# Batch 0's first DFT stage on four 64x64 tiles, and the array between the two stages stored in the order in which it is made

## The chip, the core and the metric

The kernel runs on one NeuronCore of one Trainium2 chip. The metric is the device time of one execution in microseconds (us), less is better. "Before" is the kernel without the change.

## What is computed

A frequency-domain layer feeds a feed-forward layer with a rational activation. Cut to what matters:

```python
# x: (4, 3008, 256); w_r, w_i: (256, 256); moe_w_in: (256, 2048); moe_w_out: (2048, 256)
X = np.fft.rfft(x, axis=1)
Yr = Xr @ w_r - Xi @ w_i + b_r
Yi = Xr @ w_i + Xi @ w_r + b_i
Y = soft_threshold(Yr, 0.01) + 1j * soft_threshold(Yi, 0.01)
x2 = np.fft.irfft(Y, n=3008, axis=1).reshape(12032, 256)
h = x2 @ w_in
g = (a0 + a1*h + a2*h**2 + a3*h**3) / (1 + |b0|*|h| + |b1|*h**2 + 1e-6)
out = g @ w_out
```

## The kernel before

The transform of length 3008 is split as 47 x 64, and done with matmuls for each of the four batches:

- **Stage f1** (`f1_first` for batch 0, `f1_task` for the others) is a DFT of length 47 over `n2`, for each of the 64 values of `n1`. `n1` is cut into two groups of 32 (`NG`, `NJ`), and each group into eight chunks of four (`c`). A chunk `xin` holds 2 x 47 rows (each padded to 48) by 4 x 256 columns. Its result `a` goes to `s1`, an array in DRAM.
- **Stage f2** (`f2_task`) reads `s1` back with another axis on the partitions (`load_all` into `b_all` for batch 0, `load_b` for the others): 128 partitions are 2 (real, imaginary) x 64 values of `n1`. It is a matmul with the table `f2`, 24 planes `k` in 12 pairs `p`. Batch 0's loads of `b_all` wait for all stores of `s1`, since each plane has rows from every chunk.
- **Mix** (`m_task`), soft threshold, and the **inverse stages** (`i1_task` to DRAM array `s2`, `i2_task`) follow.
- The **feed-forward part** is the main loop over 208 units `u` (26 blocks of 4 or 5 x 94 tokens, 8 units each), lines L460 (first product) to L553 (second product). The transforms of batches 1 to 3 are interleaved with it by a budget of costs.

Batch 0's transform is the prologue, written out by hand. All loads and stores of it are issued on SP's queue in program order; only `f1o`, batch 0's first table, is issued on ACT's. In order: nine warming matmuls on a tile of zeros (`warm(9)`, L625), the eight loads of `xin` (L152), four small loads (`load_small`, L636 to L640), the 16 steps of `f1_first` with a store of `a` after every second one (L187), two loads (`load_f2(0, 8)`, eight planes of the table `f2`, and `load_wt`, the mixing weights `wt`), three loads of `b_all`, more table loads, and the first raw weights of the feed-forward part (`more_raw`). `warm(WARM)`, 33 matmuls, keeps TensorE at work between the two stages. Then comes the loop over `p`, in which `f2_task`, `m_task` and `i1_task` of different `p` follow each other, with steps of `convert` between them: it turns raw 64-bit weights into pairs of 32-bit ones, 16 jobs of five steps (ACT, VectorE, GpSimd). `HC` and `HM` say how many steps stand after `f2_task` and after `m_task` of each `p`, and `HF` how many after the five first-stage tasks of batch 1 behind the loop.

`f1_first` uses one 96 x 128 table, block-diagonal over the two groups, so that one matmul does both groups for two of the four columns of a chunk. `f1_task` uses a 64 x 64 table at two places, and four matmuls on the four quarters of the array:

```python
        for g, h in ((0, 0), (1, 1), (0, 1), (1, 0)):
            r = slice(64 * g, 64 * g + 48)
            nc.tensor.matmul(out=pts[g][64 * h:64 * h + 64], lhsT=f1[r],
                             rhs=xin[b, c][r, 2 * h:2 * h + 2, :].rearrange("p j d -> p (j d)"), start=True, stop=True)
```

`copy(0, ...)` is ACT's, `copy(1, ...)` VectorE's (L159, L157). `bank` gives accumulator banks: two of tag `ft`, two of tag `h` during the prologue.

Of the kernel before, what the change touches and what calls it, by code (L numbers as in the profile page):

```python
# [29 lines left out]
HC = (0, 0, 3, 3, 3, 3, 3, 3, 3, 3, 3, 3)  # L30
HM = (0, 0, 3, 4, 3, 4, 3, 4, 3, 4, 3, 4, 8, 0)
HF = (2, 3, 2, 0, 0)
# [5 lines left out]
def dft_tables():  # L38
# [35 lines left out]
    f1o = np.zeros((NG, ROWS, NK, 2, NG))  # L74
    for q in range(NG):
        f1o[q, :, :, :, q] = f1
    f1o = np.pad(f1o.reshape(96, 96), ((0, 0), (0, 32)))
# [10 lines left out]
    sel[2:4, 130:] = 1.0  # L88
    f = np.float32
    return {  # L90
        "f1": f1p.astype(f),
        "f1o": f1o.astype(f),
        "i2": i2p.astype(f),
        "f2": f2.reshape(128, NK * 128).astype(f),
# [7 lines left out]
def spectral_moe(ctx, tc, t, out):  # L102
# [20 lines left out]
    wsp = {}  # L123
# [18 lines left out]
    def load_x(b, c):  # L142
# [8 lines left out]
        rows = 96 if b == 0 and c < 2 else 128  # L151
        nc.sync.dma_start(out=xt[:rows], in_=(t["x"][b - 1, c] if b else t["x0"][c])[:rows])  # L152
# [15 lines left out]
    a_t = {}  # L168

    def new_s1(b):  # L170
        s1[b] = dram.tile([NK, 2, NG, NJ, D], F32, tag="s1", name="s1")

    def f1_first(i):
        c, r = divmod(i, 2)
        if i == 0:
            new_s1(0)
        pt = bank(0, "f1" if r else "")
        nc.tensor.matmul(out=pt, lhsT=f1o, rhs=xin[0, c][:96, 2 * r:2 * r + 2, :].rearrange("p j d -> p (j d)"),  # L178
                         start=True, stop=True)
        if not r:  # L180
            a_t[0] = const.tile([128, 4, D], F32, tag=f"wsp{c}", name="a")[:96]
        copy(r, a_t[0][:, 2 * r:2 * r + 2].rearrange("p j d -> p (j d)"), pt[:96])
        if r:
            del xin[0, c]
        if r or i >= 14:
            z = slice(2 * r, 2 * r + 2) if i >= 14 else slice(0, 4)
            nc.sync.dma_start(out=s1[0].rearrange("k c g j d -> (k c g) j d")[:, 4 * c + z.start:4 * c + z.stop, :], in_=a_t[0][:, z])  # L187

    def f1_task(b, c, pos):
# [3 lines left out]
        for g, h in ((0, 0), (1, 1), (0, 1), (1, 0)):  # L193
            r = slice(64 * g, 64 * g + 48)
            nc.tensor.matmul(out=pts[g][64 * h:64 * h + 64], lhsT=f1[r],  # L195
                             rhs=xin[b, c][r, 2 * h:2 * h + 2, :].rearrange("p j d -> p (j d)"), start=True, stop=True)
# [17 lines left out]
        dst = s1[b].rearrange("k c g j d -> (k c) g j d")  # L214

        def send():
            for h in range(2):
                r, o = slice(64 * h, 64 * h + 48), slice(4 * c + 2 * h, 4 * c + 2 * h + 2)
                if whole is not None:
                    nc.sync.dma_start(out=dst[:, :, o], in_=whole[r])  # L220
                else:
                    for g in range(NG):
                        nc.sync.dma_start(out=dst[:, g, o], in_=parts[g][r])
# [7 lines left out]
    def load_b(b, p):  # L231
        bt = sm.tile([128, 2, D], F32, tag="b", name="bt")
        nc.sync.dma_start(out=bt, in_=s1[b][2 * p:2 * p + 2].rearrange("k c g j d -> (c g j) k d"))
        b_t[b, p] = bt
# [378 lines left out]
    with tc.manual_schedule():  # L613
        nc.vector.memset(cb, 1.0)
        f1o = pro.tile([96, 128], F32, tag="f1o", name="f1o", bufs=1)
        nc.scalar.dma_start(out=f1o, in_=t["f1o"])
# [79 lines left out]
        def load_all(k, m):  # L696
            nc.sync.dma_start(out=b_all[k // 6][:, k % 6:k % 6 + m], in_=s1[0][k:k + m].rearrange("k c g j d -> (c g j) k d"))
# [16 lines left out]
        for i in range(16):  # L714
            f1_first(i)
# [228 lines left out]
```

## Time and profile before

| | |
|---|---|
| time, median of 3 runs | 1415.99 us (1415.75 to 1417.21) |
| the profiled execution: its own time, its span | 1419.05 us, 1417.3 us |
| TensorE matmul busy | 1390.0 us, 98% of the span |
| VectorE, ACT, GpSimd busy | 91%, 81%, 47% |
| first matmul of f1, of f2 (batch 0) | 5.61 us, 29.65 us |

The span is the part of the profiled execution from its first to its last instruction. The runs without a profile are some 3 us shorter than the profiled one. In the views, PE is TensorE's matmul, PEld its weight load, DVE VectorE, SPq the sequencer of the SP queue; `L187` is a line of the program; `out<-in` names tiles without their numbers. "Landing" is the time from the issue of a transfer until its completion is seen.

### The profile page before, as it was taken

The page shows a single profiled execution, that of the slowest core. Times are in us where ns is not written, and L with a number is a line of the kernel's source. Part 1 is how long each engine was busy: PE and PEld are TensorE (multiplying, and loading weights), DVE is VectorE, ACT ScalarE, POOL GpSimd, SP SyncE. Part 2 cuts the span into 40 slices and gives each one's busy share as a digit, 9 for nine tenths or more (in the row PEclk, how much of TensorE's full clock was granted, in tenths as well). Part 3 has the DMA queues.
Part 4 walks back from the last instruction along what each step waited for, and adds up shares of the span by engine and source line. Part 5 has one row for each costly group of instructions (what it writes and reads, how often), then busy time and mean ns, then how long its engine had stood idle before and what let it go on. Part 6 is the DMA issues. An engine that isn't in the chain of part 4 may idle for free.

```text
span 1417.3 us, 20378 instructions
## 1 busy us (share of the span) xinstructions
PE 1390.0 (98%) x7279; PEld 1210.9 (85%) x7279; DVE 1291.5 (91%) x1304; ACT 1144.5 (81%) x1513; POOL 670.5 (47%) x444
## 2 busy tenths in 40 slices
PE   9998999999999999999999999999999999999997
PEld 4977889998878989898888899998888888888887
DVE  3779899898999989999989999999999999999998
ACT  2768887887888778888888778888888898888985
POOL 0444444444554444454545444444545555555553
PEclk9999999999999999999999999999999999999999
DMA  9966556556776556556687465656555465555543
GB/s 309 379 215 162 117 121 150 110 114 158 160 204 151 116 130 141 117 121 156 148 208 158 98 142 126 127 115 133 108 127 118 97 122 96 112 118 99 117 77 80
DMA packets 95657, 200.48 MB, mean 141 GB/s; under 512 B 10748, under 2 KB 51748, under 8 KB 95556
## 3 DMA queue, kind: packets, MB, share of 16 engines
q0 software_dynamic: 29664, 97.62, 38.0%
q1 hardware_dynamic: 65780, 101.51, 23.2%
q8 instruction: 58, 0.95, 0.3%
q14 instruction: 43, 0.35, 0.1%
q10 hardware_dynamic: 112, 0.05, 0.0%
HBM read 54.61 MB, written 37.49 MB: 65 GB/s over the span
## 4 chain that ended last, share of the span: by engine, by line
PE 72%; DVE 10%; issue 9%; ACT 5%; DMA 4%; SPq 0%; DVEq 0%; ACTq 0%
PE h L460 28%; PE acc L553 27%; PE pi L426 4%; PE pft L315 4%; DVE t L511 3%; DVE v L523 3%; PE pft L376 2%; DMA v<-s 2%; PE pft L297 2%; PE pft L255 2%; PE pft L195 1%; PE pft L178 1%; DVE g L520 1%; ACT t L499 1%; DMA s<-zt 1%
## 5 line engine op out<-in xcount | busy, mean ns | idle before, releaser
L553 PE MATMUL acc<-g,wsp 128*128 128x470 f32 (+1 forms) x2496 | 563.7, 375 | 3.4 <-DVE g L533 3.4
L527 POOL TENSOR_TENSOR t<-t,v 128x940 f32<-128x940 f32 (+1 forms) x206 | 469.7, 2280 | 164.4 <-DVE v L523 143.8
L553 PEld LDWEIGHTS acc<-g,wsp 128*128 128x128 f32 x2496 | 470.0, 190 | 62.8 <-DVE g L533 5.0
L460 PE MATMUL h<-xsh,win 128*128 128x470 f32 (+1 forms) x1664 | 436.9, 384 | 6.0 <-DVE t L512 5.6
L497 POOL DMA_DIRECT2D v<-s x206 | 181.6, 882 | 489.7 <-issue 452.9
L460 PEld LDWEIGHTS h<-xsh,win 128*128 128x128 f32 x1664 | 304.8, 189 | 61.6 <-PE acc L553 9.8
L520 DVE SCALAR_TENSOR_TENSOR g<-t,small,y 128x940 fp32r<-128x940 f32 (+1 forms) x208 | 250.3, 1203 | 45.8 <-ACT y L506 42.6
L492 ACT ACTIVATE v<-h 128x940 f32<-128x940 f32 (+1 forms) x208 | 196.2, 943 | 95.4 <-PE h L460 92.1
L511 DVE TENSOR_TENSOR t<-t,h 128x940 f32<-128x940 f32 (+1 forms) x208 | 231.3, 1112 | 27.3 <-ACT t L499 25.6
L512 DVE SCALAR_TENSOR_TENSOR t<-t,small,h 128x940 f32<-128x940 f32 (+1 forms) x208 | 245.2, 1179 | 7.4
L533 DVE SCALAR_TENSOR_TENSOR g<-t,small,y 128x940 fp32r<-128x940 f32 (+1 forms) x208 | 244.2, 1174 | 0.1
L460 PE MATMUL h<-xsl,win 128*128 128x470 f32 (+1 forms) x832 | 241.4, 371 | 0.0
L523 DVE SCALAR_TENSOR_TENSOR v<-v,g 128x940 f32<-128x940 f32 (+1 forms) x208 | 231.8, 1114 | 0.1
L504 ACT ACTIVATE y<-v 128x940 f32<-128x940 f32 (+1 forms) x208 | 206.1, 991 | 21.4 <-DMA v<-s 21.4
L499 ACT ACTIVATE t<-h,small 128x940 f32<-128x940 f32 (+1 forms) x208 | 216.2, 1039 | 0.0
L506 ACT ACTIVATE y<-y 128x940 f32<-128x940 f32 (+1 forms) x208 | 205.1, 986 | 2.0
L493 ACT ACTIVATE s<-h 128x940 f32<-128x940 f32 (+1 forms) x208 | 195.7, 941 | 0.0
L460 PEld LDWEIGHTS h<-xsl,win 128*128 128x128 f32 x832 | 155.8, 188 | 20.1
L426 PEld LDWEIGHTS pi<-small,ct 96*128 96x128 f32 x516 | 65.2, 192 | 7.9 <-ACT s L493 3.6
L426 PE MATMUL pi<-small,ct 96*128 96x94 f32 (+1 forms) x516 | 66.2, 275 | 3.5 <-DVE x L268 2.9
L159 ACT ACTIVATE pft<-offset 128x256 f32<-128x256 f32 x36 | 14.1, 391 | 57.6 <-DVE yt L321 23.3
L255 PEld LDWEIGHTS pft<-f,bt 128*128 128x128 f32 x288 | 37.3, 191 | 4.9 <-DVE yt L321 1.9
(113 smaller groups left out, 1071.0 us busy)
## 6 DMA issues: line engine op xcount, KB each, us to landing
v<-s POOLq DMA_DIRECT2D x190, 470.0 KB, 4.7
xin<-in_x SPq DMA_DIRECT2D x30, 512.0 KB, 6.4
s<-zt SPq DMA_DIRECT2D x48, 256.0 KB, 3.5
out_t<-ob SPq DMA_DIRECT2D x48, 235.0 KB, 4.5
ct<-s SPq DMA_DIRECT2D x20, 480.0 KB, 5.6
bt<-s SPq DMA_DIRECT2D x36, 256.0 KB, 3.3
y<-yt SPq DMA_DIRECT2D x144, 64.0 KB, 2.3
s<-a SPq DMA_DIRECT2D x46, 192.0 KB, 5.1
```

The source lines that it names most:

```text
L460: nc.tensor.matmul(out=h[:, i, :w], lhsT=l, rhs=r, start=k == 0, stop=k == len(halves) // FU - 1)
L492: nc.scalar.activation(out=d["v"], in_=h, func=ACTF.Abs, scale=rate["b0"])
L499: nc.scalar.activation(out=d["t"], in_=h, func=ACTF.Identity, scale=rate["a3"], bias=ca[:, 2:3])
L504: nc.scalar.activation(out=d["y"], in_=d["v"], func=ACTF.Square, bias=C0)
L506: nc.scalar.activation(out=d["y"], in_=d["y"], func=ACTF.Abs_reciprocal_sqrt)
L511: nc.vector.tensor_tensor(out=tt, in0=tt, in1=h, op=ALU.mult)
L512: nc.vector.scalar_tensor_tensor(out=tt, in0=tt, scalar=ca[:, 1:2], in1=h, op0=ALU.add, op1=ALU.mult)
L520: stt(out=hi, in0=tt, scalar=ca[:, 0:1], in1=y, op0=ALU.add, op1=ALU.mult)
L523: stt(out=v, in0=v, scalar=C0, in1=v32(hi), op0=ALU.add, op1=ALU.mult)
L527: nc.gpsimd.tensor_tensor(out=tt[:, :cut], in0=tt[:, :cut], in1=v[:, :cut], op=ALU.subtract)
L533: stt(out=lo, in0=tt, scalar=ca[:, 0:1], in1=y, op0=ALU.add, op1=ALU.mult)
L553: nc.tensor.matmul(out=acc[n][e][:, :w], lhsT=l, rhs=r, start=begun[n][e] == 1, stop=begun[n][e] == 3 * FU * UB)
```

## The change

Batch 0's first stage now does what `f1_task` does: per chunk four matmuls on quarters of the array (`f1_mm`, shared by both), two accumulator banks, one copy each by ACT and VectorE, two stores of 48 rows. The table `f1o` is gone; `f1` is loaded in its place at the start. All chunks of all batches are loaded as 112 rows (two groups of 48 at partitions 0 and 64); before, batch 0's first two loads had 96 rows and all others 128. `s1` has its 64 values of `n1` in the order in which the chunks give them, so that a store row is 4 KB in one piece, and the rows of the table `f2` are put in the same order on the host. The small loads go from SP's queue to ACT's. Of `f2`, four planes instead of eight are loaded ahead of `b_all`, and eight instead of four behind. The steps of `convert` start one `p` later and are spread anew.

```diff
-HC = (0, 0, 3, 3, 3, 3, 3, 3, 3, 3, 3, 3)
-HM = (0, 0, 3, 4, 3, 4, 3, 4, 3, 4, 3, 4, 8, 0)
-HF = (2, 3, 2, 0, 0)
+HC = (0, 0, 0, 3, 3, 3, 3, 3, 3, 3, 3, 3)
+HM = (0, 0, 0, 4, 4, 4, 4, 4, 4, 4, 4, 4, 8, 0)
+HF = (2, 3, 2, 1, 1)
...
+    order = np.arange(N1).reshape(NG, NJ // 4, 2, 2).transpose(1, 2, 0, 3).ravel()
...
-        "f2": f2.reshape(128, NK * 128).astype(f),
+        "f2": f2[:, order].reshape(128, NK * 128).astype(f),
...
-        rows = 96 if b == 0 and c < 2 else 128
-        nc.sync.dma_start(out=xt[:rows], in_=(t["x"][b - 1, c] if b else t["x0"][c])[:rows])
+        nc.sync.dma_start(out=xt[:112], in_=t["x"][b, c, :112])
...
-        s1[b] = dram.tile([NK, 2, NG, NJ, D], F32, tag="s1", name="s1")
+        s1[b] = dram.tile([NK, 2, N1, D], F32, tag="s1", name="s1")
...
-    def f1_first(i):
-        c, r = divmod(i, 2)
-        if i == 0:
-            new_s1(0)
-        pt = bank(0, "f1" if r else "")
-        nc.tensor.matmul(out=pt, lhsT=f1o, rhs=xin[0, c][:96, 2 * r:2 * r + 2, :].rearrange("p j d -> p (j d)"),
-                         start=True, stop=True)
-        if not r:
-            a_t[0] = const.tile([128, 4, D], F32, tag=f"wsp{c}", name="a")[:96]
-        copy(r, a_t[0][:, 2 * r:2 * r + 2].rearrange("p j d -> p (j d)"), pt[:96])
-        if r:
-            del xin[0, c]
-        if r or i >= 14:
-            z = slice(2 * r, 2 * r + 2) if i >= 14 else slice(0, 4)
-            nc.sync.dma_start(out=s1[0].rearrange("k c g j d -> (k c g) j d")[:, 4 * c + z.start:4 * c + z.stop, :], in_=a_t[0][:, z])
+    def f1_first(c):
+        if c == 0:
+            new_s1(0)
+        pts = [bank(0, "f1" if g else "") for g in range(NG)]
+        f1_mm(0, c, pts)
+        whole = const.tile([128, NG, 2, D], F32, tag=f"wsp{c}", name="a")
+        for g in range(NG):
+            copy(g, whole[:, g].rearrange("p j d -> p (j d)"), pts[g])
+        del xin[0, c]
+        dst = s1[0].rearrange("k c n d -> (k c) n d")
+        for h in range(2):
+            nc.sync.dma_start(out=dst[:, 8 * c + 4 * h:8 * c + 4 * h + 4], in_=whole[64 * h:64 * h + 48].rearrange("p g j d -> p (g j) d"))
...
-                    nc.sync.dma_start(out=dst[:, :, o], in_=whole[r])
+                    nc.sync.dma_start(out=dst[:, o:o + 4], in_=whole[r].rearrange("p g j d -> p (g j) d"))
...
-        nc.scalar.dma_start(out=f1o, in_=t["f1o"])
+        nc.scalar.dma_start(out=f1, in_=t["f1"])
...
-            nc.sync.dma_start(out=sel, in_=t["sel"])
+            nc.scalar.dma_start(out=sel, in_=t["sel"])
...
-                nc.sync.dma_start(out=bsb[2 * k:2 * k + 2, :],
+                nc.scalar.dma_start(out=bsb[2 * k:2 * k + 2, :],
...
-            nc.sync.dma_start(out=eye, in_=t["minus"])
+            nc.scalar.dma_start(out=eye, in_=t["minus"])
...
-        for i in range(16):
-            f1_first(i)
-            if i in (9, 11, 13, 15):
+        for c in range(8):
+            f1_first(c)
+            if c >= 4:
                 next(small_steps, None)
-        load_f2(0, 8)
+        load_f2(0, 4)
         load_wt()
...
-        load_f2(8, 12)
+        load_f2(4, 12)
```

## Rows read from the trace of the kernel before

**Rows 1.** The page: busy time of each engine over the whole span.

```profile
PE 1390.0 (98%) x7279; PEld 1210.9 (85%) x7279; DVE 1291.5 (91%) x1304; ACT 1144.5 (81%) x1513; POOL 670.5 (47%) x444
```

**Rows 2.** Stretches of 5 us: engines, granted clock, share of DMA engines, GB/s.

```profile
0.00:5.00 5.00, 3.77 (x9) 1.20 (x9) 0.33 (x2) 1.49 (x2) 0.20 (x4) 1.00 0.59 153
5.00:10.00 5.00, 4.64 (x7) 1.91 (x7) 0.57 (x1) 0.59 (x1) 0.00 (x0) 1.00 1.02 368
10.00:15.00 5.00, 5.00 (x13) 2.22 (x12) 1.62 (x4) 1.78 (x3) 0.00 (x0) 1.00 1.03 410
15.00:20.00 5.00, 5.00 (x13) 2.28 (x12) 3.15 (x9) 1.97 (x4) 0.00 (x0) 1.00 0.83 282
20.00:25.00 5.00, 5.00 (x21) 2.06 (x21) 2.82 (x6) 0.59 (x1) 0.00 (x0) 1.00 0.87 247
25.00:30.00 5.00, 4.16 (x21) 1.93 (x20) 0.54 (x1) 1.15 (x2) 0.00 (x0) 1.00 0.96 346
```

**Rows 3.** Timeline, 0 to 60 us, TensorE: start, duration, engine, line.

```profile
1.23 4.02 PE L625 MATMUL pft<-offset 128*128 128x512 bf16 x9 [1.23 <-DVE offset L619]
...
5.61 16.08 PE L178 MATMUL pft<-xin,f1o 96*128 96x512 f32 x32 [0.36 <-DMA f1o<-in_f1o]
...
21.53 7.29 PE L625 MATMUL pft<-offset 128*128 128x512 bf16 x33
...
29.65 1.13 PE L255 MATMUL pft<-f,b_all 128*128 128x128 f32 x8 [0.84 <-ACT wrh L661]
...
32.15 1.05 PE L255 MATMUL pft<-f,b_all 128*128 128x128 f32 x8
```

**Rows 4.** Timeline of SP's queue from the start to 130 us.

```profile
0.74 5.17 SPq L152 DMA_DIRECT2D xin<-in_x  x8
...
9.42 0.36 SPq L640 DMA_DIRECT2D eye<-in_minus  x1
10.78 11.97 SPq L187 DMA_DIRECT2D s<-a  x9
22.80 0.43 SPq L700 DMA_DIRECT2D f<-in_f  x1
23.28 0.46 SPq L709 DMA_DIRECT2D wt<-in_w  x1
25.17 1.40 SPq L697 DMA_DIRECT2D b_all<-s  x3
```

**Rows 5.** Waits of SP's queue, 0 to 24 us: total, times, longest.

```profile
SPq L152 <- DMA f1o<-in_f1o: 1.6, 1, 1.6
SPq L638 <- DMA xin<-in_x: 1.5, 2, 0.8
SPq L640 <- DMA xin<-in_x: 1.0, 1, 1.0
```

**Rows 6.** The timeline at batch 1's first stage, which has the four tiles.

```profile
94.59 3.01 PE L195 MATMUL pft<-xin,small 48*64 48x512 f32 x24
```

**Rows 7.** Batch 0's `a`: copies, issues (ns min/median/max), landing of the stores.

```profile
L187 SPq DMA_DIRECT2D s<-a x9: 303/304/319, 10.8 to 22.4; - x9
L159 ACT ACTIVATE a<-pft x8: 592/592/593, 7.7 to 20.9; 96x512 f32<-96x512 f32 x8
L157 DVE COPY a<-pft x8: 686/686/687, 9.4 to 21.7; 96x512 f32<-96x512 f32 x8
...
DMA to landing us min/median/max: 2.7/3.4/4.9
```

**Rows 8.** Line L223, stores of 48 rows: issue in ns, min/median/max.

```profile
L223 SPq DMA_DIRECT2D s<-a x8: 368/420/834, 106.0 to 109.6; - x8
```

**Rows 9.** Line L233, loads of 256 KB back from `s1`: landing.

```profile
DMA to landing us min/median/max: 2.7/3.3/7.9
```

**Rows 10.** Waits of all engines, 30 to 104 us: total, times, longest.

```profile
ACT e L597 <- DMA raw_win<-in_w_in: 3.4, 1, 3.4
PE pft L376 <- DVE x L276: 1.6, 2, 1.1
```

More of the change, by code (lines that the diff above doesn't have):

```diff
@@ L73, in dft_tables @@
     g[1, :, :, 1] = cot * wi.T[:, :, None]
[L74 to L77, printed above, removed]
     f1p = np.zeros((NG, 64, 64))
@@ L166, in flush, with f1_mm @@
             late.pop(0)()
-    a_t = {}
     def new_s1(b):
-        s1[b] = dram.tile([NK, 2, NG, NJ, D], F32, tag="s1", name="s1")
-    def f1_first(i):
-        c, r = divmod(i, 2)
-        if i == 0:
-            new_s1(0)
-        pt = bank(0, "f1" if r else "")
-        nc.tensor.matmul(out=pt, lhsT=f1o, rhs=xin[0, c][:96, 2 * r:2 * r + 2, :].rearrange("p j d -> p (j d)"),
-                         start=True, stop=True)
-        if not r:
-            a_t[0] = const.tile([128, 4, D], F32, tag=f"wsp{c}", name="a")[:96]
-        copy(r, a_t[0][:, 2 * r:2 * r + 2].rearrange("p j d -> p (j d)"), pt[:96])
-        if r:
-            del xin[0, c]
-        if r or i >= 14:
-            z = slice(2 * r, 2 * r + 2) if i >= 14 else slice(0, 4)
-            nc.sync.dma_start(out=s1[0].rearrange("k c g j d -> (k c g) j d")[:, 4 * c + z.start:4 * c + z.stop, :], in_=a_t[0][:, z])
+        s1[b] = dram.tile([NK, 2, N1, D], F32, tag="s1", name="s1")
+    def f1_mm(b, c, pts):
+        for g, h in ((0, 0), (1, 1), (0, 1), (1, 0)):
+            r = slice(64 * g, 64 * g + 48)
+            nc.tensor.matmul(out=pts[g][64 * h:64 * h + 64], lhsT=f1[r],
+                             rhs=xin[b, c][r, 2 * h:2 * h + 2, :].rearrange("p j d -> p (j d)"), start=True, stop=True)
+    def f1_first(c):
+        if c == 0:
+            new_s1(0)
+        pts = [bank(0, "f1" if g else "") for g in range(NG)]
[7 more added lines that the diff above has]
+            nc.sync.dma_start(out=dst[:, 8 * c + 4 * h:8 * c + 4 * h + 4], in_=whole[64 * h:64 * h + 48].rearrange("p g j d -> p (g j) d"))
     def f1_task(b, c, pos):
@@ L192, in f1_task @@
         pts = [bank(b, "f1" if g else "m" if 4 <= pos < 6 else "") for g in range(NG)]
[L193 to L196, printed above, removed]
+        f1_mm(b, c, pts)
         yield
@@ L232, in load_b @@
         bt = sm.tile([128, 2, D], F32, tag="b", name="bt")
-        nc.sync.dma_start(out=bt, in_=s1[b][2 * p:2 * p + 2].rearrange("k c g j d -> (c g j) k d"))
+        nc.sync.dma_start(out=bt, in_=s1[b][2 * p:2 * p + 2].rearrange("k c n d -> (c n) k d"))
         b_t[b, p] = bt
@@ L696, in load_all @@
         def load_all(k, m):
-            nc.sync.dma_start(out=b_all[k // 6][:, k % 6:k % 6 + m], in_=s1[0][k:k + m].rearrange("k c g j d -> (c g j) k d"))
+            nc.sync.dma_start(out=b_all[k // 6][:, k % 6:k % 6 + m], in_=s1[0][k:k + m].rearrange("k c n d -> (c n) k d"))
         def load_f2(a, z):
@@ L751, in spectral_moe @@
                 nc.sync.dma_start(out=i2, in_=t["i2"])
-                nc.sync.dma_start(out=f1, in_=t["f1"])
             if p >= 1:
@@ L924 @@
     for g in range(NG):
-        xg = x.reshape(B, N2, NG, NJ // 4, 4, D)[:, :, g].swapaxes(1, 2)
-        xp[0, :, g * ROWS:g * ROWS + N2] = xg[0]
-        xp[1:, :, g * 64:g * 64 + N2] = xg[1:]
-    arrays = {"x": xp[1:], "x0": xp[0], **dft_tables()}
+        xp[:, :, g * 64:g * 64 + N2] = x.reshape(B, N2, NG, NJ // 4, 4, D)[:, :, g].swapaxes(1, 2)
+    arrays = {"x": xp, **dft_tables()}
     w = np.stack([inputs[n] for n in ("w_r", "w_i")])
```

8 lines of the change are left out of this document (3 added, 5 removed).

## The prediction

> **What bounds the kernel now.** The page comes first: TensorE is busy for 98% of the span [rows 1], and behind the prologue the change alters no matmul, copy or count of elements. There each unit can only move as a whole: what the prologue's end gains or loses, the end of the kernel gains or loses. So the question is when batch 0's second stage starts, and whether the loop over `p` keeps that.
>
> The stretches of 5 us show the start [rows 2]. Summed, the DMA engines have moved 0.77 MB by 5 us, 2.6 by 10 and 4.65 by 15 us, at 410 GB/s when full. From 15 to 25 us they fall to 282 and 247 GB/s. The timeline says why [rows 3]: L178, 32 instructions for 16 matmuls, runs from 5.61 to 21.69 us without a gap. TensorE paces the first stage, the stores follow it, and the DMA engines idle in part. Then the second stage waits. The last store is issued at the end of a row that reaches from 10.78 to 22.75 us, and the first load of `b_all`, which waits for every store's landing, goes out at 25.17 us [rows 4]. L255 starts at 29.65 us. Its wait is put down to ACT's `wrh`, which `f2_task` does not read; I read it as the landing of `b_all`, 4.5 us after its issue, behind `f2` and `wt` (1.05 MB by the code) on the same queue.
>
> SP's waits show one more thing [rows 5]: the eighth load of `xin`, the ninth transfer, waited for `f1o`, the first; the two biases, 11th and 12th, and `eye`, the 13th, waited for `xin`. Every transfer waits for the one eight before it, counted over both queues. `eye` is issued at 9.42 us after such a wait [rows 4], so the fourth `xin` landed then.
>
> **The change, part by part.**
>
> *Loads of x.* By the code 2 x 96 + 6 x 128 rows of 4 KB, 3.93 MB, become 8 x 112 rows, 3.67 MB; the first four hold 1.84 MB either way. No row shows a load of 112 rows; between those of 96 and 128 rows I take its bytes. The fourth lands at 9.4 us as before; the DMA engines had moved its 1.9 MB by 5 + 1.13/0.368 = 8.1 us [rows 2], so a landing is 1.3 us behind its bytes. The later four (2.33, 2.79, 3.25, 3.70 MB with what is small) then land at 10.6, 11.8, 12.9 and 14.0 us.
>
> *Small loads on ACT's queue.* They are now the 10th to 13th transfers on an engine that runs in order, so they wait for the first four `xin`. Behind them stand ACT's copies. ACT is held until 9.4 + 0.4 (issue) = 9.8 us, its first copy ends at 10.4 us, and as it has two banks, the third chunk's matmuls start at 10.45 us. Before, this wait was SP's, whose first store went at 10.78 us.
>
> *Matmuls.* Three chunks on four tiles take 3.01 us [rows 6], 1.0 each, where L178 took 16.08 us for eight chunks [rows 3], 2.0 each. With the copies of 0.59 and 0.69 us [rows 7] and two banks a chunk follows each 0.9 us: the last ends at 10.45 + 5 x 0.9 + 1.0 = 16.0 us, 5.7 us before the old end. The first two run at half pace whatever comes: 7 matmul records in 5 to 10 us, 13 in each 5 us after [rows 2], while the granted clock reads 1.00 (2.4 GHz) in all of them.
>
> *Stores.* 16 instead of 9. The first four are the 14th to 17th transfers and wait for the last four `xin`: 10.65, 11.8, 12.9, 14.0 us. The other twelve follow at SP's pace. Their issue is not in the trace; the same shape in 96 rows is 0.304 us [rows 7], 48 rows of 2 KB are 0.42 us, at most 0.834 [rows 8]. At 0.35 to 0.45 the last goes at about 19 us, and the DMA engines are behind it: twelve stores are 2.36 MB, 5.8 us at 410 GB/s, to 20.1 us. The least landing was 2.7 us for 0.39 MB [rows 7], of which 1.0 is its bytes, so the last store has landed at 20.1 + 1.8 = 21.9 us. `b_all` is issued at 22.0 instead of 25.17 us. At 0.834 us per issue the last store would go at 24 us and this gain would be gone.
>
> *Two loads ahead of `b_all`.* 0.79 instead of 1.05 MB, queued right behind the stores; they run from 20.1 to 22.0 us, while the last stores' landing is awaited. So `b_all` meets an empty queue: 3.3 us [rows 9] instead of 4.5. The second stage starts at 22.0 + 3.3 = 25.3 us, 4.35 us earlier than 29.65.
>
> *The eight planes of `f2` behind.* The third `f2_task` starts 2.5 us after the first [rows 3], at 27.8 us. Its planes are in a load of 0.52 MB behind 0.79 MB of `b_all` from 22.0 us: bytes to 25.3, landing 27.1 to 28.6 us. Between nothing and 0.8 us I take 0.35 lost.
>
> *Warming matmuls.* Unchanged, 7.3 us [rows 3]: they run from 16.0 to 23.3 us, and TensorE is then idle for 2.0 us where it was 0.84. Cost zero if the pace holds; else see the second rival.
>
> *Conversions.* The sum stays 80 steps. The six of `p` = 2, where ACT waited 3.4 us for raw weights [rows 10], go to the later `p`, seven each instead of six or seven, and two come behind the loop. Written out step by step, VectorE has the same conversion work as before ahead of the third of `HF`'s copies, and one step more among the last two, where ACT's copies and VectorE's have some room. TensorE's waits for VectorE's `x` are 1.6 us in the whole loop [rows 10]; a step more in a `p` can add some, removing the wait of 3.4 us can take some. Between -1 and +1 us I take zero.
>
> *Layout and the permuted table.* Same loads back; a store of the later batches is 4 KB rows. TensorE waits for none of them in the shown rows; zero.
>
> Sum: 4.35 - 0.35 = 4.0 us. From the profiled execution's 1419.05 us (span 1417.3) that is 1415.05; the runs without a profile stand 3.06 us under it, so 1415.99 - 4.0 = 1412.0 us. What this kernel's measurement can tell from no change is about 0.2%, 2.8 us: below 1413.2 it is faster, above 1418.8 slower.
>
> **The Trainium skill against it.** "DMA: Bandwidth & Descriptors", under "Rules for kernel authors", says that two transfers to disjoint partition halves run one behind the other on the same engines, and that one transfer should be made of them; the change does the opposite with its stores. That is the third rival. "TensorE: Matmul & The Clock Gate", in Part 1, says that a TensorE left idle falls back to 1.2 GHz; no row here shows a fall, and that is the second.
>
> **Rivals.**
>
> *The loop does not keep it (chance 0.13).* The conversions start with the first raw weights, which ACT awaited for 3.4 us [rows 10]. The DMA engines are nearly full then (346 GB/s, share 0.96) [rows 2]. For it: if the raw weights land when they did, ACT, in order, is held in the fourth `p` and half of the gain goes. Against it: 0.26 MB less of x stands in front of them. 1414.0 us.
>
> *The pace falls between warming and second stage (0.08).* For it: matmuls ran at half pace from 1.23 to near 10 us [rows 2, 3], so a new rise might take as long. Against it: 2.0 us is a short gap. Half pace over 4 us costs 2 us: 1414.0 us.
>
> *The halves cost (0.06).* Eight stores more, each with some 1.7 us beside its bytes [rows 7], over eight in flight: 8 x 1.7 / 8 = 1.7 us; 1413.7 us. For it: the transfers wait in turn. Against it: the queue is full meanwhile.
>
> *Slower: the first stage stays at half pace (0.06).* The first two chunks, at half pace (1.75 us each, twice their pitch), end at 9.1 us, and TensorE idles until 10.45 us, while ACT is held. If it then stays at half pace, the last chunk ends at 10.45 + 6 x 1.75 = 20.95 us, and the 33 warming matmuls at 4.02 / 9 = 0.45 us [rows 3] end at 35.8 us, 6.1 us after the old start: 1422.1 us. It decides from some 18 of the 33 at half pace (20.95 + 7.3 + 18 x 0.23 = 32.4 us, 2.8 us late). Against it: the first rise came some 8 us after the first matmul, and from 10.45 us that is 18.5.
>
> **How the numbers follow.** The forecast has 0.67, and its own bounds (stores' issue, the third `f2_task`, one us of the loop each way) give 1410 to 1413.2. The three rivals without a loss have 0.27 and end at 1413.7 to 1414; the slower one has 0.06. Faster 0.67, within 0.2% 0.27, slower 0.06. A range of 8 in 10 takes in the first three rivals with half a us beyond them, and half a us more of gain: 1409.5 to 1414.9.
>
> **What would show it.** ACT's first copy near 10 us, last matmul of the first stage near 16, `b_all`'s first issue near 22.0 and L255's start near 25.3 us; DMA over 380 GB/s from 5 to 22 us; in the loop the same waits. Wrong would be: stores that take 0.6 us to issue, a late second stage behind the warming matmuls, or a gain at 25 us that is gone at the main loop's first L460 matmul.

## The result, and the profile after

The changed kernel takes 1423.85 us (median of 6 runs, 1421.67 to 1426.08) beside 1416.08 us for the kernel before: a ratio of 1.0053, interval 1.0040 to 1.0066. It is slower, by 7.5 us at the ratio. The prediction was 1412.0 us. A ratio here is the comparison's own figure with its 95% interval, and need not be the quotient of the two medians.

The page of the changed kernel, beside [rows 1]: TensorE is busy 1.5 us less, in a span of 1423.1 us that is 5.8 us longer. So TensorE stands idle 7.3 us more.

```profile
PE 1388.5 (98%) x7309; PEld 1210.2 (85%) x7311; DVE 1293.2 (91%) x1304; ACT 1145.9 (81%) x1513; POOL 669.8 (47%) x444
```

The stretches of 5 us, columns as in [rows 2]:

```profile
5.00:10.00 5.00, 3.29 (x25) 0.68 (x24) 1.39 (x2) 1.19 (x2) 0.00 (x0) 1.00 1.06 256
10.00:15.00 5.00, 2.56 (x24) 0.66 (x24) 2.20 (x5) 1.79 (x3) 0.00 (x0) 1.00 1.04 252
15.00:20.00 5.00, 4.17 (x29) 1.11 (x26) 3.94 (x12) 1.99 (x4) 0.00 (x0) 1.00 1.02 357
25.00:30.00 5.00, 1.12 (x6) 0.29 (x3) 0.00 (x0) 0.44 (x1) 0.00 (x0) 0.95 0.88 287
30.00:35.00 5.00, 3.98 (x17) 3.59 (x18) 2.41 (x4) 1.30 (x3) 0.00 (x0) 0.50 0.96 303
```

From 5 to 15 us the DMA engines are full (share 1.04 to 1.06) and yet move only 252 to 256 GB/s; in [rows 2] it was over 360. TensorE is busy for 5.85 of these 10 us. From 30 us the granted clock is 0.50, the lower of its two levels (1.2 GHz). The timeline of TensorE, beside [rows 3]:

```profile
5.64 1.09 PE L170 MATMUL pft<-xin,small 48*64 48x512 f32 x8 [0.40 <-DMA small<-in_f]
7.35 1.09 PE L170 MATMUL pft<-xin,small 48*64 48x512 f32 x8 [0.62 <-DMA xin<-in_x]
...
16.65 2.24 PE L170 MATMUL pft<-xin,small 48*64 48x512 f32 x16 [0.72 <-ACT a L154]
18.83 7.29 PE L618 MATMUL pft<-offset 128*128 128x512 bf16 x32
31.02 2.04 PE L249 MATMUL pft<-f,b_all 128*128 128x128 f32 x8 [4.89 <-DMA b_all<-s]
...
40.08 1.06 PE L249 MATMUL pft<-f,b_all 128*128 128x128 f32 x8
```

A chunk takes 1.09 us, but one begins only each 1.8 us, which is the time of a chunk's 458,752 bytes (112 rows of 4 KB) at 255 GB/s: the loads of x set the pace. (Some of these waits are put down to ACT's copy of the chunk before, which ends just ahead of them; the last chunk follows without such a wait.) The stage still ends 2.8 us earlier than in [rows 3], at 18.9 us. Then the gain is lost: the second stage begins at 31.02 us instead of 29.65, after 4.89 us of idleness, and its first task takes 2.04 us, at half pace. The fourth `f2_task` starts 9.1 us after the first. In the kernel before it was 6.5, from 29.65 us [rows 3] to this row of its timeline:

```profile
36.16 1.06 PE L255 MATMUL pft<-f,b_all 128*128 128x128 f32 x8
```

The timeline of SP, beside [rows 4], then two of SP's waits, beside [rows 5] (engine, line, what it waited for; us in total, times, longest):

```profile
8.62 15.26 SPq L184 DMA_DIRECT2D s<-a  x16
...
26.60 1.40 SPq L690 DMA_DIRECT2D b_all<-s  x3
```

```profile
SPq L184 <- DMA xin<-in_x: 6.4, 5, 1.5
SPq L147 <- DMA small<-in_f: 3.5, 1, 3.5
```

The 16 stores go out over 15.26 us, until 23.9 us. `b_all` follows at 26.60 us. ACT's timeline shows that the small loads did not hold it: they were issued at once, ahead of x's fourth load, and the first copy ran at 6.78 us.

```profile
1.26 0.51 ACTq L629 DMA_DIRECT2D sel<-in_sel  x1
...
2.37 0.36 ACTq L633 DMA_DIRECT2D eye<-in_minus  x1
...
6.78 0.60 ACT L154 ACTIVATE a<-pft 128x512 f32<-128x512 f32 x1 [4.09 <-PE pft L170]
```

They took four of the eight turns that the prediction had given to x; x's fourth load now waits 3.5 us for the table `f1`. Where the loop over `p` ends, one more wait stands in the timeline of TensorE, for `yt`, the soft-thresholded planes that `i1_task` reads, and the granted clock is 0.50 from 98 to 101 us. The first matmul of the main loop (L454) starts at 109.6 us; L460 of the kernel before started at 102.7.

```profile
97.75 2.08 PE L370 MATMUL pft<-yt,g 128*128 128x256 f32 x4 [1.49 <-DVE yt L361]
```

### The profile page after: what moved, and what is told of

It is laid out like the page before. It is cut to its first block, busy times and chain, and to the rows that moved or that the text cites. A ratio compares the mean times of both kernels' runs of the same rounds, so it can differ in the third digit from the quotient of the medians.

```text
span 1423.1 us, 20443 instructions
## 1 busy us (share of the span) xinstructions
PE 1388.5 (98%) x7309; PEld 1210.2 (85%) x7311; DVE 1293.2 (91%) x1304; ACT 1145.9 (81%) x1513; POOL 669.8 (47%) x444
## 4 chain that ended last, share of the span: by engine, by line
PE 73%; DVE 11%; issue 9%; ACT 5%; DMA 3%; SPq 0%; DVEq 0%; ACTq 0%; POOLq 0%
PE h L454 28%; PE acc L547 27%; PE pft L309 4%; PE pi L420 4%; DVE t L505 3%; DVE v L517 3%; PE pft L249 3%; PE pft L370 3%; PE pft L291 2%; PE pft L170 2%; DMA v<-s 1%; PE pm L352 1%; DVE g L514 1%; ACT t L493 1%; DVE g L527 1%
## 5 line engine op out<-in xcount | busy, mean ns | idle before, releaser
L454 PE MATMUL h<-xsh,win 128*128 128x470 f32 (+1 forms) x1664 | 437.7, 385 | 6.8 <-DVE t L506 5.5
L454 PEld LDWEIGHTS h<-xsh,win 128*128 128x128 f32 x1664 | 305.8, 190 | 62.7 <-PE acc L547 9.9
L454 PE MATMUL h<-xsl,win 128*128 128x470 f32 (+1 forms) x832 | 241.8, 372 | 0.0
L454 PEld LDWEIGHTS h<-xsl,win 128*128 128x128 f32 x832 | 156.1, 188 | 20.1
L154 ACT ACTIVATE pft<-offset 128x256 f32<-128x256 f32 x36 | 14.1, 392 | 57.0 <-DVE yt L315 22.7
```

Of the source, the lines that this page charges most:

```text
L454: nc.tensor.matmul(out=h[:, i, :w], lhsT=l, rhs=r, start=k == 0, stop=k == len(halves) // FU - 1)
```

## The experiments

The kernel before had medians from 1415.8 to 1417.3 us in these comparisons. The half loads are a single run.

### How many rows a load has

All loads of x in the changed kernel with 128 rows; each of its loads of 112 split in two of 48; and the first two loads of the kernel before with 128 instead of 96.

```diff
-        nc.sync.dma_start(out=xt[:112], in_=t["x"][b, c, :112])
+        nc.sync.dma_start(out=xt, in_=t["x"][b, c])                 # 128 rows
...
+        for g in range(NG):                                         # half loads
+            nc.sync.dma_start(out=xt[64 * g:64 * g + 48], in_=t["x"][b, c, 64 * g:64 * g + 48])
```

> The kernel after the change, with all loads of x in 128 rows instead of 112 (16 rows of zeros more per chunk, never read). In the trace of after, the DMA engines move a flat 250 to 258 GB/s at a busy share of 1.04 from 5 to 16 us, while the 112-row loads run, and 410 to 422 GB/s from 17 to 21 us, with stores alone; in the trace of before 222 to 242 GB/s from 4 to 6 us (two 96-row loads) and 410 from 7 us on (128-row loads). Theory 'row count': loads of 112 (and 96) rows are slow by themselves. Then here over 380 GB/s from 7 us on, last matmul of the first stage near 15 instead of 18.8 us, first issue of b_all near 22.5 instead of 26.6 us, and some 3 to 6 us less in all: 1418 to 1421 us. Rival 'few loads in flight' (the small loads on ACT's queue take turns that the loads of x had, so that the fourth load of x is issued only when the table has landed): the rate stays near 255 GB/s and the time near 1424 us.

> The kernel after the change, with each chunk of x loaded in two transfers of 48 rows (partitions 0 to 47 and 64 to 111) instead of one of 112; the rows between are not loaded. A look at the rate from 5 to 12 us. Theory 'rows per engine': any load that isn't 128 rows is slow, so about 250 GB/s here as well, while stores of 48 rows ran at 410 to 422. Rival: 112 and 96 are slow for another reason (their count), and 48 rows load at 380 GB/s or more.

> The kernel before the change, with its first two loads in 128 rows instead of 96. By the theory 'row count' the stretch at 222 to 242 GB/s from 4 to 6 us goes, and the first two chunks land 0.5 to 1 us earlier; TensorE's 16 matmuls pace that stage, so 0 to 1 us of it is left: 1415 to 1416 us. Rival: the first table, not x, is what the first matmul awaits (5.57 us in before), and nothing changes at all.

One us of each while x is loaded, in the order changed kernel, 128 rows, half loads, and kernel before while its 96-row loads run; columns as in [rows 2]:

```profile
10.00:11.00 1.00, 0.22 (x4) 0.00 (x0) 0.69 (x1) 0.60 (x1) 0.00 (x0) 1.00 1.05 250
```

```profile
10.00:11.00 1.00, 0.43 (x5) 0.00 (x0) 0.48 (x1) 0.53 (x1) 0.00 (x0) 1.00 1.04 381
```

```profile
10.00:11.00 1.00, 1.00 (x6) 0.19 (x6) 0.00 (x0) 0.00 (x0) 0.00 (x0) 1.00 1.05 184
```

```profile
5.00:6.00 1.00, 0.64 (x2) 0.39 (x2) 0.00 (x0) 0.00 (x0) 0.00 (x0) 1.00 1.04 242
...
8.00:9.00 1.00, 1.00 (x2) 0.34 (x1) 0.00 (x0) 0.31 (x1) 0.00 (x0) 1.00 1.04 414
```

At the same full share a load moves 381 to 414 GB/s with 128 rows, 250 with 112, 242 with 96 and 184 with 48. It is not the engines' number that differs, since all are busy. The kernel before had this slow rate too, from 4 to 6 us; stretches of 5 us had averaged it away. In the time: 1421.87 us, 1.0037 (1.0025 to 1.0050) with 128 rows, 2.3 us less than the change, where the theory had 3 to 6 and the two intervals overlap. The rate came as the theory had it, but the first stage ended only at 18.3 us, since the granted clock fell to 0.50 within it, from 11.4 to 18 us. The half loads took 1426.32 us, and 184 GB/s is less than either side had expected. With its first two loads in 128 rows the kernel before takes 1416.73 us, 1.0007 (0.9998 to 1.0016), which cannot be told from no change.

### The steps of convert

The changed kernel with the old `HC`, `HM`, `HF`; the kernel before with the new; and the latter with two steps moved behind the loop, or two from there to `HM`.

```diff
 HC = (0, 0, 0, 3, 3, 3, 3, 3, 3, 3, 3, 3)
 HM = (0, 0, 0, 4, 4, 4, 4, 4, 4, 4, 4, 4, 8, 0)    # two later: 6, two earlier: 10
 HF = (2, 3, 2, 1, 1)                               # two later: 2, 2, two earlier: 0, 0
```

> The kernel after the change, with HC, HM and HF of before. Theory 'steps': in after, the inverse stage at the loop's end waits for ACT copies that stand behind one conversion step more (89 to 98 us), TensorE idles 1.5 us, the granted clock falls to 0.50 from 97.9 to 101.3 us, and from the 14th p to the main loop's first matmul 3.4 us more are lost than at the 14th p itself (2.6 us). With the old steps that part is as before: about 3 us less, 1420.5 us. Rival: the end of the loop is late for the start's sake, and the order of steps is worth under 0.5 us: 1423.5 us.

> The kernel before the change, with HC, HM and HF of after, and nothing else. Theory 'steps': the new order loses 2 to 3 us at the loop's end, 1418 to 1419 us. Rival 'the order is free': within 0.5 us of 1416 us. A gain, 1415 us, if removing ACT's wait of 3.4 us for raw weights counts.

> The kernel before with the new steps of convert, of which two are moved from the m_task of the last place with steps (8 to 6) to behind the fourth and fifth of the tasks behind the loop (1, 1 to 2, 2). With the new steps alone the kernel before took 3.0 us more, and TensorE waited 1.49 us for VectorE's yt ahead of the last i1_task, where it waits 0.50 us with the old steps. Theory (the steps in front of that i1_task hold ACT and VectorE, and so yt): the wait falls to 0.5 us and the ratio from 1.0021 to 1.0012 or below. Rival (all steps late by one place cost somewhere behind): the wait moves on to the tasks behind the loop and the ratio stays at 1.002.

> The kernel before with the new steps of convert, of which the two behind the loop (fourth and fifth task) are moved to the m_task of the last place with steps (8 to 10), so that as in the kernel before seven steps stand behind the loop. Two steps moved the other way made the ratio 1.0047 where the new steps alone had 1.0021. Theory (steps behind the loop cost, where TensorE has little else to do and waits for the copies): the ratio falls to 1.0010 or below. Rival (the steps ahead of the last i1_task cost, by a longer wait for yt there): TensorE's wait for yt grows from 1.49 us beyond 2 us and the ratio stays at 1.002 or above.

| kernel | us | ratio |
|---|---|---|
| changed, old steps | 1419.17 | 1.0024 (1.0014 to 1.0034) |
| before, new steps | 1417.84 | 1.0021 (1.0010 to 1.0032) |
| before, new steps, two later | 1423.41 | 1.0047 (1.0033 to 1.0060) |
| before, new steps, two earlier | 1418.11 | 1.0014 (1.0003 to 1.0025) |

The steps are worth 4.1 us inside the change and 3.0 us alone. The traces place this in the loop: from the fourth `f2_task` to the main loop's first matmul the changed kernel takes 69.5 us, and 64.8 with the old steps; the kernel before takes 66.5 and, in a second profile (below), 64.9, and 68.1 with the new steps. TensorE's waits from 80 to 115 us, first with the new steps, then two later, then two earlier:

```profile
PE pft L376 <- DVE yt L367: 1.5, 1, 1.5
PE h L460 <- ACT xsh L429: 0.9, 1, 0.9
```

```profile
PE h L460 <- ACT xsh L429: 2.0, 1, 2.0
PE pft L195 <- DVE a L157: 1.2, 1, 1.2
PE pft L376 <- DVE yt L367: 0.6, 1, 0.6
```

```profile
PE pft L376 <- DVE yt L367: 1.5, 1, 1.5
PE h L460 <- DVE t L512: 0.5, 1, 0.5
```

Two later: the wait for `yt` does fall to 0.6 us, as the theory had it, but it comes back behind the loop as waits for the copies `a` and `xsh` (the main loop's first operand), and the time rises by another 3.7 us at the ratios. So the rival's mechanism holds, though it had expected the same ratio. Not all of the 3.7 us need be these waits: in this trace the granted clock is 0.50 from 106 to 110 us, behind the wait for `xsh`, and also from 30 to 32 us, ahead of the first step of `convert`. Two earlier: the wait for `yt` stays at 1.5 us and does not grow, as the rival had said it would, and the one for `xsh` falls from 0.9 to 0.2 us; the ratio of 1.0014 lies between the two expectations. Of the 3.0 us, some 2.0 are left with the two steps moved back, and so go with the later start of the steps; that the two steps behind the loop make the rest is inside the intervals. That the steps delay the copies because ACT and VectorE are at work on them is how I read these waits; which step delays which copy was not tried.

### The clock

More warming matmuls in the changed kernel; then 128 rows and the old steps together; and this with two matmuls on zeros behind each of the first seven chunks and 48 warming ones.

```diff
-WARM = 33
+WARM = 57            # the filled version: 48
...
             f1_first(c)
+            if c < 7:                    # the filled version only
+                warm(2, "m")
```

> The kernel after the change, with 57 warming matmuls instead of 33, so that they end near 31.3 us, when the second stage's data are there (31.0 us in the trace of after). Theory 'clock': in after the granted clock fell to 0.50 from 29.8 to 36.3 us, after 4.9 us without a matmul, and cost 2.5 us (third f2_task to fourth). Without the gap it stays at 1.00, the fourth f2_task starts near 37.8 instead of 40.1 us, and the kernel takes 2 to 2.5 us less: 1421.5 us. Rival 'the loop is bound elsewhere' (conversions, DMA): the fourth f2_task is earlier, but at the end nothing is left of it: 1423.5 to 1424 us.

> The kernel after the change, with both single edits that gained: all loads of x in 128 rows (2.0 us by medians) and HC, HM, HF of before (4.7 us). Theory 'separate costs': they add up, 1423.85 - 6.7 = 1417.2 us, still not under 1416, since the granted clock still falls, in the first stage or behind the warming matmuls. Rival 'one cost': both cure the same late start, and together give no more than the old steps alone, 1419 us.

> The kernel of both edits (128 rows, old steps) and in addition two warming matmuls after each of the first seven chunks of the first stage, and 48 instead of 33 between the stages. Theory 'clock': in the run with 128 rows alone the granted clock was 0.50 from 11.4 to 18 us and from 28.3 to 35 us, after gaps of 0.5 to 0.9 us between the chunks and one of 3.5 us behind the warming matmuls. Without these gaps it stays at 1.00, the first stage ends near 15.5 us, the second starts near 26.5 us and the fourth f2_task near 33 us (36.2 before): 1412.5 to 1414 us, faster than before by 2 to 3 us. Rival 'the data are late': the clock stays up, but b_all lands near 29 us as it did (stores), and nothing is gained on before: 1416 to 1417 us.

With 57: 1424.54 us, 1.0067 (1.0055 to 1.0079). The gap between the stages is closed, but the clock had fallen within the first stage, behind the gaps of 0.7 to 1.1 us between its first four chunks, and stayed at 0.50 until 21 us; the stage ended at 20.8 us, and the 57 matmuls behind it held TensorE until 33.5 us, so that the fourth `f2_task` came at 39.9 us, as late as without them. One us of that stage:

```profile
12.00:13.00 1.00, 1.00 (x8) 0.00 (x0) 0.00 (x0) 0.00 (x0) 0.00 (x0) 0.50 1.03 233
```

The 128-row version and the one with the old steps show the same fall within the first stage, at 11 to 12 us.

128 rows with the old steps: 1419.37 us, 1.0028 (1.0016 to 1.0039), no better than the old steps alone, so the two do not add. The filled version: 1.00 granted through the whole start of the traced execution, which took 1421.14 us; the median is 1419.57 us, 1.0026 (1.0016 to 1.0035). Keeping the clock at the start gains nothing more than the old steps did.

The granted clock also differs between executions of one kernel. Of the twelve of the filled version with the small loads on SP's queue (next section), five with a mean clock of 0.998 or 0.999 took 1417.65 to 1419.55 us, and seven with 0.995 to 0.997 took 1421.84 to 1424.31 us. The six of the changed kernel have 0.991 to 0.997, the 20 of the kernel before beside the first experiments 0.995 to 1.000. That speaks for falls of the clock as a part of the 7.5 us; how large a part was not separated from the waits that go with them.

### The stores

With loads, steps and clock as they were, 3.7 us remain. Each store of the kernel before in two halves of 48 rows; the filled version with the small loads on SP's queue; with two chunks merged in a store; with every second store on ACT's queue; with whole stores of 128 rows; and with the old layout of `s1`.

```diff
# kernel before, half stores
+            for h in (slice(0, 48), slice(48, 96)):
+                nc.sync.dma_start(out=s1[0].rearrange("k c g j d -> (k c g) j d")[h, 4 * c + z.start:4 * c + z.stop, :], in_=a_t[0][h, z])
# two queues
-            nc.sync.dma_start(out=dst[:, 8 * c + 4 * h:...
+            (nc.scalar if h else nc.sync).dma_start(out=dst[:, 8 * c + 4 * h:...
# pairs: one store of 48 rows x 8 KB for two chunks, collected in g1[:, :16] or f2[:, 8:24]
+        whole = (f2[:, 8:24] if c // 2 % 2 else g1[:, :16]).rearrange("p (n j e) f -> p n (j e f)", n=4, j=2)
# whole stores: s1 with 8 planes more, 16 padding rows of each half stored too
+        dst = s1[0].rearrange("k c (z h n) d -> z h (k c) (n d)", h=2, n=4)
+        nc.sync.dma_start(out=dst[c], in_=whole.rearrange("p g j d -> p (g j d)"))
```

> The kernel before with one edit: each of its first-stage stores is issued as two of 48 rows (partitions 0 to 47, 48 to 95). Theory: the stores of halves are what the best version of the change still loses; in runs of the new stage with whole 128-row loads 16 half stores went out until 22.4 to 23.0 us and the first load of b_all at 25.7 to 26.1 us, in runs of the kernel before with other edits at 23.4 to 23.7 us. So here b_all goes out near 25.5 to 26 us where the stage itself is the old one, and the time is 1417.5 to 1419 us. Rival: half stores only fill idle turns of the queue; b_all stays at 23.4 to 25.2 us and the time at 1416 us.

> The same filled version with the four small loads on SP's queue again, behind the loads of x as in the kernel before. Theory: on ACT's queue they are issued at 1.3 to 2.4 us and take turns ahead of x's fourth load; moved back, the loads of x go out earlier and the time falls by 0.3 to 1 us, to 1418.6 to 1419.2 us. Rival: what they gain the stores behind them lose, 1419.6 us.

> The filled version of the new stage (128-row loads, old conversion steps, two matmuls more after each of the first seven chunks, 48 warming matmuls) with its stores merged: two chunks are collected in one tile, and each half of it goes out as one store of 48 rows x 8 KB, 8 stores instead of 16; the rows of the table f2 are permuted to fit. Theory (number of half stores): the last store goes out near 18 us, b_all near 22.5 to 23.5 us, the second stage starts at 27 to 27.5 us unless the 48 warming matmuls run longer, and the time falls from 1419.6 to 1416 to 1417.5 us. Rival (bytes, not number): the same bytes take the same time, b_all stays near 25.7 us and the time at 1419.5 us.

> The filled version with the small loads on SP's queue, and of each chunk's two half stores the second issued on ACT's queue. Before it the 16 stores went out on SP's queue in 12.8 us (9.88 to 22.75 us), while the stage's matmuls ended at 16.9 us. Theory (the DMA engines are the bound: 230 to 290 GB/s at a share of 0.74 to 1.0 from 15 to 25 us): the issue is spread but b_all goes out within 0.7 us of 25.5 us and the time is the same, a ratio of 1.0026. Rival (SP's issue of the stores, one waiting behind the other): the last store goes out near 19 us, b_all at 23 us, and 2 us are gained, a ratio of 1.0010.

> The filled version with the small loads on SP's queue, and one store of 128 rows for each chunk in place of two of 48: the array s1 gets room for the 16 padding rows of each half, which are stored too, so 8 stores move 4.19 MB where 16 moved 3.15 MB. Theory (two stores of a part of the partitions are what costs): whole-width stores run near the 410 GB/s of the whole-width loads, the last one is issued before 20 us, b_all goes out at 23 to 24.5 us instead of 25.5, and the ratio falls from 1.0026 to 1.0015 or below, a third more bytes notwithstanding. Rival (bytes into the array at the 230 to 290 GB/s seen behind the loads): 4.19 MB take 15 us, b_all goes out at 27 to 28 us and the ratio is 1.004 to 1.005.

> The filled version of the new stage (128-row loads, old conversion steps, no gaps between the chunks) with the array s1 and the rows of the table f2 in the old order again, for all four batches: a half store is then 48 rows of two pieces of 2 KB instead of one of 4 KB. It is the part of the change that was not tried yet; the filled version stands 3.5 to 3.7 us over the kernel before, of which half stores gave 2.2 us in the kernel before. Theory: the layout is worth nothing to the half stores or to the later batches, so that the time stays at a ratio of 1.0026 (1419.5 to 1420.5 us beside 1416 to 1417). Rival: the remaining 1.5 us are the new layout's, and the ratio falls to 1.0015.

| kernel | us | ratio |
|---|---|---|
| before, half stores | 1419.46 | 1.0015 (1.0003 to 1.0027) |
| filled, small loads on SP's queue | 1422.00 | 1.0026 (1.0014 to 1.0039) |
| filled, pairs | 1423.25 | 1.0039 (1.0025 to 1.0052) |
| filled, two queues | 1423.80 | 1.0051 (1.0035 to 1.0068) |
| filled, whole stores | 1488.33 | 1.0497 (1.0482 to 1.0513) |
| filled, old layout | 1421.09 | 1.0032 (1.0019 to 1.0044) |

Half stores alone cost the kernel before 2.1 us (0.4 to 3.8). Its TensorE and SP timelines: the stage ends at 20.1 us, `b_all` goes out at 24.93 us, which is still in the rival's range, and TensorE waits 3.14 us for it. Then the granted clock is 0.50 from 32 to 34 us, and the fourth `f2_task` starts at 38.50 us, where it is 36.16 and 35.68 in the two profiles of the kernel before.

```profile
5.21 14.88 PE L178 MATMUL pft<-xin,f1o 96*128 96x512 f32 x32
...
30.35 1.54 PE L256 MATMUL pft<-f,b_all 128*128 128x128 f32 x8 [3.14 <-DMA b_all<-s]
```

```profile
10.35 12.67 SPq L188 DMA_DIRECT2D s<-a  x18
...
24.93 1.44 SPq L698 DMA_DIRECT2D b_all<-s  x3
```

SP's waits say what the halves changed. In the kernel before, SP waited for VectorE's copies before most of its stores, and issued each store in 0.30 us:

```profile
SPq L187 <- DVE a L157: 8.4, 7, 1.4
```

In its second profile (below), with a shorter first stage, that wait is 3.5 us. With half stores no wait for VectorE's copies is left, 0.7 us for ACT's are, and an issue takes up to 1.07 us: the stores have fallen behind TensorE by themselves.

The filled version with the small loads on SP's queue shows best where the early end goes. Its trace is of the fastest of its twelve executions, 1417.65 us beside a median of 1422.00. TensorE, SP, the issues of its stores (ns, min/median/max), and the two stretches behind the loads of x:

```profile
15.80 1.09 PE L170 MATMUL pft<-xin,small 48*64 48x512 f32 x8
16.82 10.53 PE L618 MATMUL pft<-offset 128*128 128x512 bf16 x48
29.78 1.13 PE L249 MATMUL pft<-f,b_all 128*128 128x128 f32 x8 [2.42 <-DMA b_all<-s]
```

```profile
9.88 12.82 SPq L184 DMA_DIRECT2D s<-a  x16
...
25.50 1.40 SPq L690 DMA_DIRECT2D b_all<-s  x3
```

```profile
L184 SPq DMA_DIRECT2D s<-a x16: 302/416/1447, 9.9 to 21.7; - x16
```

```profile
15.00:20.00 5.00, 5.00 (x29) 1.80 (x26) 2.84 (x7) 1.20 (x2) 0.00 (x0) 1.00 0.84 250
20.00:25.00 5.00, 5.00 (x25) 2.25 (x23) 0.00 (x0) 0.00 (x0) 0.00 (x0) 1.00 0.88 262
```

Here the first stage ends at 16.9 us, 4.8 us earlier than in [rows 3], and `b_all` still goes out at 25.50 us. Between them the DMA engines move 250 to 262 GB/s at a share of 0.84 to 0.88, SP waits for no copy, and its last twelve stores take 0.65 us each to issue: the stores, not TensorE, set the end. As a theory for the small loads this run failed (no gain). Its second stage begins at 29.78 us, only 0.1 us behind [rows 3], and this execution is as fast as the kernel before: what the median loses is not in this trace. Pairs tell nothing on the number of stores: the third pair waits for the first one's landing, since both use one tile, and TensorE with it:

```profile
18.64 1.56 PE L170 MATMUL pft<-xin,small 48*64 48x512 f32 x8 [3.82 <-ACT g L154]
```

Two queues: 233 GB/s from 15 to 20 us at a share of 0.91 with both queues issuing, and `b_all` at 27.11 us, which speaks against SP's issue as the limit. It is no clean test: `b_all` was later by 1.6 us, more than the 0.7 us that the theory allowed. SP's small loads waited 4.4 us for the landing of ACT's stores, so that SP's first store went out at 14.77 us instead of 9.88, and two of ACT's copies stood behind stores that waited in turn. Whole stores failed in their own way, in a stretch of 5 us:

```profile
15.00:20.00 5.00, 5.00 (x32) 1.71 (x25) 3.05 (x8) 1.20 (x2) 0.00 (x0) 1.00 0.14 56
```

A share of 0.13 to 0.14 is two engines of 16: this store's array in DRAM is written with the two halves as its outermost dimension. So this run says nothing on halves. The Trainium skill, "DMA: Bandwidth & Descriptors", section "Why a DMA increments its semaphore by 16 and not by 1", says that a transfer uses the largest number of engines up to 16 that divides the outermost dimensions of both sides; the 0.13 agrees. By the same rule loads of 112, 96 and 48 rows have all 16 engines, and their shares of 1.04 agree; that their rate falls with the rows is not in it.

The old layout changes nothing that can be told (1.0032 beside 1.0026), so the 3.7 us are not the layout's.

### Planes of f2 ahead of b_all, and the kernel before once more

```diff
-        load_f2(0, 8)
+        load_f2(0, 4)
...
-        load_f2(8, 12)
+        load_f2(4, 12)
```

> The kernel before with one edit: four planes of the table f2 instead of eight are loaded ahead of b_all, eight instead of four behind. Theory: the transfers ahead of b_all end in the time in which the last stores' landing is awaited, so that the edit moves the second stage by less than 0.7 us and the third f2_task's wait for its planes gives that back; 1415.5 to 1416.5 us. Rival (the prediction's): b_all meets an emptier queue and lands about 1 us sooner, 1415 us; or the eight planes behind come late for the third f2_task and it loses 1 us or more, 1417 us.

> The kernel before, unchanged, with a second profile. Theory: the profiled execution that the prediction rests on was a late one of a scatter of its own (its first 32 weight loads and matmuls took 16.08 us, while two other kernels with the same first stage took 14.0 us); a second one shows some 14 to 15 us for L178, b_all issued at 23.4 to 25.2 us, and the same ratio, 1.0000 within 0.0012. Rival: 16 us again and b_all at 25.2 us, which would make the difference to those other kernels one of their edits.

The split alone: 1416.42 us, 0.9993 (0.9982 to 1.0003), no difference that can be told. Its TensorE timeline shows both sides: the second stage begins 3.8 us after `b_all`'s issue at 25.47 us, and the third `f2_task` then waits for its planes:

```profile
29.30 1.13 PE L255 MATMUL pft<-f,b_all 128*128 128x128 f32 x8 [0.34 <-issue]
...
33.41 1.13 PE L255 MATMUL pft<-f,b_all 128*128 128x128 f32 x8 [1.42 <-DMA f<-in_f]
```

The kernel before again: 1416.55 us, 0.9998 (0.9989 to 1.0007). Its second profile has a first stage of 14.00 us, not 16.08 [rows 3], and `b_all` at 23.64 us, not 25.17 [rows 4]:

```profile
5.65 14.00 PE L178 MATMUL pft<-xin,f1o 96*128 96x512 f32 x32 [0.90 <-DMA f1o<-in_f1o]
...
29.18 1.13 PE L255 MATMUL pft<-f,b_all 128*128 128x128 f32 x8 [2.40 <-DMA b_all<-s]
```

Its main loop starts at 100.6 us instead of 102.7, and yet its span is 1417.6 us, 0.3 us longer than 1417.3. So single profiles say little of 2 us, and the part behind the start does not move as a whole, which the prediction had taken for granted. Nor does a profile add some 3 us: this execution took 1419.38 us, 2.8 over its median, but others with a profile were 1.2 to 4.4 us under theirs (1415.52 us for the first two loads of 128 rows, 1417.70 for half stores, 1417.65 above).

## Why the prediction was wrong

It forecast a second stage at 25.3 us and a gain of 4.0 us; the stage began at 31.02 us. Step by step:

- **Stores** is the step that failed first. It took the last 12 stores at 410 GB/s and their issue at 0.35 to 0.45 us: the last out at 19 us, `b_all` at 22.0. Measured: 23.9 and 26.60 us, and with x loaded at full rate and the stage over at 16.9 us still 22.7 and 25.50, at some 230 to 290 GB/s, a share of 0.74 to 0.97 and 0.65 us for an issue. The prediction's own sign of being wrong, "stores that take 0.6 us to issue", came true. Its reading of the kernel before was right: stores followed TensorE there, since SP waited 8.4 us for VectorE's copies. What it had no row for is how 16 stores of 48 rows go once nothing holds them back; it gave them the rate of the loads. Whether the issue waits for the DMA engines, or they for the issue, stays open.
- **Loads of x** at their bytes and 410 GB/s failed: 250 to 258 GB/s, the last chunk started at 17.7 us, where the last x was to land at 14.0. The two bounds, 96 and 128 rows, stood in one stretch of 5 us, and the slow one could have been read from stretches of 1 us. Worth 2.3 us with the new steps (not clear of noise), nothing with the old.
- **Conversions**, "zero, between -1 and +1 us", measured 3.0 us alone and 4.1 inside the change, the largest single loss. Its mechanism (a step more delays a copy that TensorE needs) was named, and mis-sized.
- **Warming matmuls**: idle for 4.89 us instead of 2.0. The pace fell, as the second rival had it, and from the first to the fourth `f2_task` 2.5 us were lost; but keeping the clock (the filled version) gained nothing beyond the old steps. The slower rival's 1422.1 us lies nearest to the result, and by luck as far as the trace goes: the changed kernel's first stage ran at 1.00 there. It did fall to 0.50 in three of its versions (57 warming matmuls, 128 rows, old steps).
- **Small loads on ACT's queue**: wrong. ACT was never held; the four loads went out at 1.3 to 2.4 us, ahead of x's fourth. Moving them back ended the stage 1.1 us earlier and changed nothing in the time.
- **Two loads ahead of b_all** and **the eight planes of f2 behind**: right in kind, and they cancel. The planes cost 1.42 us in the kernel before, not 0.35.
- **Matmuls**: 1.09 us a chunk beside 1.0, right, but in the changed kernel at full pace from the first chunk on (the filled version's first chunk took 1.98 us). **Layout**: zero, right.
- **The halves cost**, a rival of 1.7 us with a chance of 0.06, came true as a cost: 2.1 us (0.4 to 3.8) in the kernel before.
- **The sum's base**: the 3.06 us between the profiled execution and the median were put down to the profile. The 20 runs of the kernel before beside the first experiments reach from 1413.75 to 1419.37 us, and the second profile, with `b_all` 1.5 us earlier, was as long: the first was one execution of a scatter. The 3.06 us cancel in the forecast.

The runs split the 7.5 us into 4.1 for the steps and 3.4 for the rest. Of the rest half stores would explain 2.1, if they cost in the new stage what they cost in the old. Whether the other 1.3 to 1.6 us exist is inside the intervals, and in the new stage itself halves could not be replaced by a clean whole store, so that part stays argued, not shown. No version tried beat the kernel before.

## What to carry to other kernels

Before costing a faster stage, ask what the stores behind it would do if nothing held them back: a stage that ends 4.8 us earlier gains nothing if what follows waits for stores at 250 GB/s. Rows in which stores wait for their copies do not show it. Read the rate in stretches of 1 us, with the DMA share beside it. Do not price a transfer by its bytes when its shape changes, and treat reordered filler work as a change of its own, timed alone. Look at two profiles of the kernel before when the effect is of the size of its scatter.

## What the runs showed of the hardware

- Loads from DRAM at a full DMA share (1.04 to 1.05) moved 381 to 414 GB/s with 128 rows of 4 KB, 250 with 112, 242 with 96, 184 with 48.
- The same 48-row stores that moved 250 GB/s in the filled version with the small loads on SP's queue ran at 410 to 422 GB/s from 17 to 21 us in the changed kernel, right behind the loads of x (and at 410 to 422 from 15 to 18 us in the filled version itself):

```profile
18.00:19.00 1.00, 1.00 (x9) 0.12 (x4) 0.96 (x3) 0.44 (x2) 0.00 (x0) 1.00 1.02 410
```

  What decides between these rates stays open. The issue of such a store took 0.30 to 1.47 us, that of a 96-row store of the kernel before 0.30 to 0.32 [rows 7], at most 0.65 in its second profile.
- A store written with an outermost dimension of 2 in DRAM ran on two engines: 52 to 56 GB/s at a share of 0.13 to 0.14, and the kernel took 71 us more than the kernel before.
- The granted clock fell to 0.50 not only after 4.89 us of idleness, but also within the first stage, in the version with 57 warming matmuls, behind three gaps of 0.7 to 1.1 us between chunks of 1.1 us. In the changed kernel itself gaps of 0.4 to 1.0 us left it at 1.00 there. After the gap of 1.49 us at the end of the loop it fell in the changed kernel (0.50 from 98 to 101 us), and after the same gap in the kernel before with the new steps it stayed at 1.00. Ahead of the second stage it fell after 2.17, 2.82 and 3.14 us of idleness (the kernel before with two steps later, two earlier, and half stores), and stayed after 2.40, 2.42 and 2.72 us (the kernel before again, the filled version with the small loads on SP's queue, the kernel before with the new steps). So the length of one gap does not tell alone.
